# A convolution and a two-layer GELU network on one core: where the last tap is multiplied, and in which order the taps are added

## The chip, the cores and the metric

The kernel runs on one core of a Trainium2 chip. The metric is the device time of one execution in microseconds (us); smaller is better. The engines are TensorE (PE in the profile, its weight loads PEld), VectorE (DVE), ScalarE (ACT), GpSimd (POOL) and SyncE (SP, which only issues DMAs here). Each engine works through a queue of its own in the order in which the program issued its instructions, and engines wait for each other by semaphores.

## The reference

```python
w = softmax(weight, axis=-1)                      # 8 heads x 7 taps
x_pad = concat([zeros((B, 6, D)), x], axis=1)     # B = 8, S = 4096, D = 192
x = einsum('hk,bskhg->bshg', w, windows(x_pad, 7)).reshape(B * S, D)
h = x @ w_in                                      # 192 -> 2048
g = h * (1.0 / (1.0 + np.exp(-1.702 * h)))
return (g @ w_out).astype(np.float32)             # 2048 -> 192
```

A causal convolution of seven taps along the sequence, with one set of weights for every head of 24 channels, is followed by a product into 2048 columns, a GELU and a product back to 192. All is float32.

## The kernel before, in words

The 32768 tokens are taken in 32 blocks ("big" = 0 to 31) of 1024 tokens. For each block:

- **Convolution.** x is loaded by eight DMAs (`load_x`, L66) and turned by VectorE into `xt` (`transpose_x`, L439), in three groups of channels c = 0, 1, 2. From block 3 on ScalarE multiplies each of the 3 x 7 taps (`tap`, L483; the multiplication is L487). Tap 0 goes straight into the block's place in `conv_t`; the others go to "homes", pieces of the large buffer `g` that the second product has done with. The taps of c = 0 are added by accumulating DMAs (`tree`, L509); those of c = 1 and c = 2 by twelve additions on GpSimd (`next_add`, L501, the addition is L504), each into `conv_t`. Before the change these wait in a list `adds`, from which the newest is taken first. When a block's additions are issued ("done"), SP copies its block 2 across the halves of the partitions (`cross`); the other blocks and eleven sums of them (`vsum`, made by GpSimd, L363) follow later as `cross` pieces.
- **First product** (`hidden`, L763). A fast matrix scheme makes it out of 20 products for each half v = 0, 1 of the columns (`product1`, L588: the matmul at L595; each is two matmuls on 64 rows, and the trace shows each as two passes). The hand-written list `FIRST` (L643) names its items in order: "prod" on TensorE, "copy" (L630) and "gelu" (L612 from PSUM, L617 from SBUF) on ScalarE, "sum" (L636, or L363 and L361) on VectorE. Names a0 to a9 are PSUM banks handed out in turn from `free`, k0 to k6 are places in `room` (SBUF). An item's first number says whose it is: 0, this half; 1, the next half; 2, the next half's opening product 11. After the second half, items 1 belong to the next block and wait in `later`: the copy a2<-a0 is issued by `seeds_ahead` during the second product (PLAN's "final"), the rest by `rest_ahead` (L733) at the beginning of the next block's first product. So a first product begins with products 0, 4, 10, 6, 2, 13, 18, and with the copies k2<-a2 (after product 0, before product 10 writes a2 again), k6<-a0 and k1<-a9; then `FIRST` begins with its half v = 0.
- `FILL` (L659; `FILL_1`, L670, for block 1) tells what else is issued ahead of which item of `FIRST`, for each half: "add" additions, "turn" transposes of the block after next (the first of them issues whatever is left of the next block's taps and additions), "vsum", "g" the early sums of g (L361, L363, L995), "tap", "cross", and, for block 1, "work", a step of the convolution on VectorE.
- **Second product** (`second`, L1001; matmuls at L1019). It, too, is a fast scheme. The list `PLAN` (L954) is its order: "main" begins one of 20 main products of four steps (one of two), "side" appends three side products, "go" n does n steps, each one step of the main product for three column groups and one matmul of a side product beside them. When a side product ends, ScalarE copies it to `room` at once (L1044, the side copy). "seed" (L1048, ScalarE) puts a value back into PSUM, "join" (VectorE, L361 or L363) adds values, "sum" makes sums of pieces of g ("spots") on VectorE and "acc" on GpSimd's DMA queue, "turn" and "store" put out results, and "tap", "tree", "vsum" and "cross" are the next block's work. "final" gives two banks free and lets `seeds_ahead` copy a2<-a0 for the next first product.

The tap homes are spots of g: 11, 10, 16 for c = 0; 17, 14, 20 for c = 1; 15, 13, 9 for c = 2 (two taps each). So a tap can be multiplied when the second product has read that spot, and a GELU of the next first product may write the spot only when the tap has been added. `need("done n")` issues everything that block n still lacks.

In PLAN before the change 20 taps are issued up to "final" and the last, tap 6 of c = 1, right behind it. The additions are issued in FILL at the items 0, 6 and 9.

Of the kernel before, what the change touches and what calls it, by code (L numbers as in the profile page):

```python
# [15 lines left out]
def kernel(  # L16
# [80 lines left out]
    g = consts.tile([P, NG, 2, 2, NG, T], F32)  # L97
# [381 lines left out]
    TAPS_IN = (0, 2, 1)  # L479
    TREE = {2: [(1, 2)], 4: [(3, 4)], 6: [(5, 6), (0, 1), (3, 5), (0, 3)]}  # L480
    TREE_1 = {2: [(1, 2)], 4: [(3, 4), (0, 1)], 6: [(5, 6), (0, 3), (0, 5)]}

    def tap(big, c, k):  # L483

        dst = own(big)[:, 2 * c : 2 * c + 2, :]
        home = tap_home(big, c, k) if k else dst
        act.mul(home, conv_src(big, c, k), cw[:, c, k : k + 1])  # L487
        if k and c not in DMA_TAPS and big > 1:
            adds.append((dst, home))
            if big == 2:  # L490
                next_add()
            return
# [6 lines left out]
    tree, adds = [], []  # L499

    def next_add():  # L501
        if adds:
            dst, home = adds.pop()
            nc.gpsimd.tensor_add(dst, dst, home)  # L504
# [133 lines left out]
    def plain(u, m, n, v, slot, ks=range(NC), first=0):  # L638

        for k in ks:  # L640
# [20 lines left out]
            0: (("add", 4),), 6: (("add", 4),), 7: (("turn", 0),), 9: (("add", 4),), 21: (("turn", 1),),  # L661
            26: (("turn", 2),),
        },
        {
            0: (("vsum",),), 1: (("vsum",), ("vsum",)), 2: (("g", 0),), 6: (("vsum",), ("vsum",)), 8: (("vsum",),),
            12: (("vsum",),), 14: (("g", 1),), 15: (("g", 2),), 17: (("vsum",), ("vsum",)), 18: (("g", 3),),
            21: (("vsum",),), 23: (("g", 4),), 25: (("vsum",),), 35: (("cross",),),
# [4 lines left out]
            0: (("add", 12),), 4: (("tap",),), 6: (("work", 0.8),), 15: (("work", 0.8),), 16: (("work", 0.8),),  # L672
            21: (("tap",),), 23: (("tap",),), 25: (("tap",), ("work", 0.8), ("work", 0.8)), 28: (("work", 0.8),),
            32: (("tap",),), 35: (("tap",),), 38: (("tap",),), 42: (("work", 0.8),),
        },
        {
            0: (("g", 0),), 6: (("g", 1),), 19: (("g", 2), ("g", 3)), 23: (("g", 4),), 25: (("turn", 0),),
            28: (("turn", 1),), 31: (("turn", 2),),
# [259 lines left out]
    def store(big, n, o=None, queues=(nc.sync,) * 3):  # L938
# [16 lines left out]
        ("sum", 14, 14, "-", 18), ("side", 13, 16, "k0"), ("main", 1, 5, "p2", 1), ("sum", 7, 8, "-", 7), ("vsum",),  # L955
# [45 lines left out]
    def second(big, bx, bs, by, final, last):  # L1001
# [74 lines left out]
        while ready and big > 1:  # L1076
            next_tap()
# [273 lines left out]
```

## Time and profile before

| | us |
|---|---|
| median of 3 runs | 2300.35 (2299.83 to 2300.5) |
| the profiled execution | 2299.75 |
| its span, first to last instruction | 2298.0 |
| TensorE busy in it | 2271.9 |

The profile's rows give a line of the kernel, an engine and an operation, what it writes and reads by the program's own names, and the shapes. In a timeline each row is a run of like instructions: its start and length in us, their count, and in brackets the idle time of the engine just before and what ended it. "issue" there means that nothing that the profile shows was waited for. In the chain of waits a row is start, length, engine, what it writes and the line.

### The profile page before, as it was taken

The numbers are of one execution on the slowest core, as the hardware profiler recorded it, in microseconds if no ns is written. First come the engines' busy times: TensorE is split into PE (matmuls) and PEld (weight loads), VectorE is DVE, ScalarE is ACT, GpSimd is POOL, SyncE is SP. The second block draws the span as 40 slices with busy tenths as digits, with TensorE's granted clock in tenths as the row PEclk, the third lists the DMA queues.
The fourth block names the chain that finished last, engine by engine and source line by source line (L and its number), as shares of the span: only waits on it lengthen the run. The fifth ranks groups of instructions, "written<-read, shape, count | busy, mean of one in ns | idle before, by whom it ended". The sixth has DMA issues, their size and how long they took to land.

```text
span 2298.0 us, 62000 instructions
## 1 busy us (share of the span) xinstructions
PE 2271.9 (99%) x24966; PEld 1377.8 (60%) x24966; DVE 1921.3 (84%) x2842; ACT 1775.9 (77%) x3481; POOL 1100.6 (48%) x1101
## 2 busy tenths in 40 slices
PE   9899999999999999999999999999999999999999
PEld 5356656666656666566666566665666655666655
DVE  8798888888888878888888888888888888888788
ACT  8578777778877787777788777877777887778755
POOL 1445554555454555545554445555455544455510
PEclk9999999999999999999999999999999999999999
DMA  8976667656666656676566666666765667664543
GB/s 198 158 150 131 127 126 150 133 124 123 131 137 138 129 122 126 127 148 135 123 123 132 138 138 128 123 124 128 148 134 123 123 130 139 139 126 99 100 98 71
DMA packets 281072, 298.84 MB, mean 130 GB/s; under 512 B 120144, under 2 KB 212304, under 8 KB 280784
## 3 DMA queue, kind: packets, MB, share of 16 engines
q0 software_dynamic: 58080, 151.48, 36.6%
q1 hardware_dynamic: 221056, 143.00, 27.4%
q8 instruction: 197, 3.23, 0.6%
q14 instruction: 91, 0.75, 0.1%
q10 hardware_dynamic: 1648, 0.39, 0.1%
HBM read 53.15 MB, written 25.17 MB: 34 GB/s over the span
## 4 chain that ended last, share of the span: by engine, by line
PE 94%; DVE 2%; DMA 1%; ACT 1%; issue 1%; SPq 0%; DVEq 0%; ACTq 0%
PE slot L595 48%; PE slot L1019 44%; PE slot L837 1%; DMA g<-in_moe_w_in_dram 1%; DVE g L363 0%; DVE g L361 0%; PE slot L842 0%; SPq L266 0%; DMA xin<-in_x_dram 0%; ACT g L612 0%; DMA w_in_s<-in_moe_w_out_dram 0%; ACT g L487 0%; DMA conv_t<-conv_t 0%; ACT room L630 0%; ACT w_form L487 0%
## 5 line engine op out<-in xcount | busy, mean ns | idle before, releaser
L595 PE MATMUL slot<-conv_t,w_in_s 64*128 64x512 f32 x5152 | 1170.6, 599 | 8.6 <-issue 4.8
L595 PEld LDWEIGHTS slot<-conv_t,w_in_s 64*128 64x128 f32 x5152 | 728.0, 186 | 440.3 <-issue 218.6
L1019 PE MATMUL slot<-g,w_form 128*32 128x256 f32 x9672 | 895.3, 379 | 0.3 <-DVE room L363 0.3
L1019 PEld LDWEIGHTS slot<-g,w_form 128*32 128x32 f32 x9672 | 482.2, 110 | 160.3 <-DVE room L363 0.8
L636 DVE TENSOR_TENSOR slot<-slot,room 128x512 f32<-128x512 f32 x496 | 321.0, 693 | 212.3 <-ACT g L612 162.5
L504 POOL TENSOR_TENSOR conv_t<-conv_t,g 128x512 f32<-128x512 f32 x354 | 452.6, 1282 | 66.8 <-ACT g L487 43.8
L612 ACT ACTIVATE g<-slot 128x512 f32<-128x512 f32 x776 | 421.1, 613 | 77.7 <-PE slot L595 77.5
L1019 PE MATMUL slot<-g,w_out_s 128*32 128x256 f32 x5952 | 467.6, 380 | 2.9 <-DVE g L363 1.5
L363 DVE TENSOR_TENSOR g<-g 128x1024 f32<-128x1024 f32 x372 | 442.8, 1224 | 1.1
L1044 ACT COPY room<-slot 32x256 f32<-32x256 f32 x651 | 237.4, 365 | 253.7 <-PE slot L1019 242.9
L630 ACT COPY room<-slot 128x512 f32<-128x512 f32 x620 | 339.9, 611 | 31.4 <-PE slot L595 19.4
L1019 PEld LDWEIGHTS slot<-g,w_out_s 128*32 128x32 f32 x5952 | 238.9, 110 | 195.4 <-ACT g L617 23.5
L487 ACT ACTIVATE g<-xt,cw 128x512 f32<-128x512 f32 x534 | 350.7, 714 | 3.0
L363 POOL TENSOR_TENSOR conv_t<-conv_t 128x256 f32<-128x256 f32 x210 | 193.5, 929 | 232.1 <-PE slot L595 186.7
L995 POOL DMA_DIRECT2D g<-g x124 | 107.6, 943 | 352.3 <-PE slot L1019 166.6
L1019 PE MATMUL slot<-osbs,w_form 128*32 128x256 f32 x2232 | 225.3, 379 | 0.1
L509 POOL DMA_DIRECT2D g<-g x120 | 104.5, 886 | 224.4 <-DVE room L363 88.5
L630 ACT COPY slot<-slot 128x512 f32<-128x512 f32 x248 | 136.5, 572 | 54.9 <-PE slot L595 52.9
L617 ACT ACTIVATE g<-room 128x1024 f32<-128x1024 f32 x124 | 132.7, 1070 | 55.2 <-DVE room L636 55.2
L636 DVE TENSOR_TENSOR slot<-room,slot 128x512 f32<-128x512 f32 x248 | 156.3, 684 | 14.7 <-PE slot L595 13.7
L636 DVE TENSOR_TENSOR room<-slot,room 128x512 f32<-128x512 f32 x248 | 158.7, 681 | 2.5 <-ACT room L630 1.8
L361 DVE TENSOR_TENSOR room<-room 96x256 f32<-96x256 f32 x155 | 87.4, 564 | 71.1 <-ACT room L1044 70.0
(171 smaller groups left out, 1772.5 us busy)
## 6 DMA issues: line engine op xcount, KB each, us to landing
g<-g POOLq DMA_DIRECT2D x124, 512.0 KB, 5.6
xin<-in_x_dram SPq DMA_DIRECT2D x240, 180.0 KB, 4.1
conv_t<-conv_t SPq DMA_DIRECT2D x186, 192.0 KB, 2.9
g<-g POOLq DMA_DIRECT2D x120, 256.0 KB, 4.5
out_dram<-osbs SPq DMA_DIRECT2D x186, 128.0 KB, 2.8
conv_t<-conv_t SPq DMA_DIRECT2D x124, 128.0 KB, 2.5
g<-room POOLq DMA_DIRECT2D x31, 512.0 KB, 5.5
conv_t<-g POOLq DMA_DIRECT2D x60, 256.0 KB, 4.2
```

What stands on the lines that cost most here:

```text
L363: eng.tensor_sub(v(dst), v(a), v(b))
L487: act.mul(home, conv_src(big, c, k), cw[:, c, k : k + 1])
L504: nc.gpsimd.tensor_add(dst, dst, home)
L509: nc.gpsimd.dma_start(out=out, in_=src, accum_op=ALU.add)
L595: nc.tensor.matmul(slot[h], w_in_s[halves[h], a, v * P : (v + 1) * P], src, start=first, stop=True, skip_group_check=True,)
L612: act.activation(dst[:, :, h, :], src[h].rearrange("p (o t) -> p o t", o=2), AF.Gelu_apprx_sigmoid, scale=float(sign),)
L617: act.activation(dst.rearrange("p o h t -> p h o t"), src.rearrange("p h (o t) -> p h o t", o=2), AF.Gelu_apprx_sigmoid, scale=float(sign),)
L630: act.copy(bank(dst, h), bank(src, h))
L636: op(*(bank(t, h) for t in (dst, a, b)))
L995: nc.gpsimd.dma_start(out=spot(dst), in_=spot(a), accum_op=ALU.add)
L1019: nc.tensor.matmul(dst, w, t, start=first, stop=last, skip_group_check=True)
L1044: act.copy(to, d)
```

## The change

Three things are altered. The last of a block's 21 taps is no longer issued in the second product: `second` now leaves two entries in `ready` (that tap and its label), and FILL issues the tap ahead of item 2 of the next `FIRST`, so behind the copies k2, k6 and k1 and the first GELU on ScalarE. The additions are no longer taken newest first but in the order of a list, `ADDS_IN`, that begins with the last tap. And the orders in `FIRST`, `FILL`, `FILL_1` and `PLAN` are written anew around that.

```diff
     TAPS_IN = (0, 2, 1)
+    ADDS_IN = [(1, 6), (2, 5), (2, 6), (2, 1), (2, 2), (2, 3), (2, 4)] + [(1, k) for k in range(1, 6)]
...
         if k and c not in DMA_TAPS and big > 1:
-            adds.append((dst, home))
+            adds.append((ADDS_IN.index((c, k)), dst, home))
+            adds.sort(key=lambda a: a[0])
...
         if adds:
-            dst, home = adds.pop()
+            _, dst, home = adds.pop(0)
             nc.gpsimd.tensor_add(dst, dst, home)
...
     FIRST = [
-        (0, "sum", "a3", "a4", "-", "k1"), (0, "gelu", 2, 1, "a0", 1), (0, "copy", "k0", "a2", 1),
...
+        (0, "gelu", 2, 1, "a0", 1), (0, "sum", "a3", "a4", "-", "k1"), (0, "copy", "k0", "a2", 1),
...
     FILL = [
         {
-            0: (("add", 4),), 6: (("add", 4),), 7: (("turn", 0),), 9: (("add", 4),), 21: (("turn", 1),),
-            26: (("turn", 2),),
+            2: (("tap",), ("add", 4)), 3: (("add", 4),), 4: (("add", 4),), 5: (("turn", 0),), 26: (("turn", 1),),
+            29: (("turn", 2),),
         },
         {
-            0: (("vsum",),), 1: (("vsum",), ("vsum",)), 2: (("g", 0),), 6: (("vsum",), ("vsum",)), 8: (("vsum",),),
-            12: (("vsum",),), 14: (("g", 1),), 15: (("g", 2),), 17: (("vsum",), ("vsum",)), 18: (("g", 3),),
-            21: (("vsum",),), 23: (("g", 4),), 25: (("vsum",),), 35: (("cross",),),
+            0: (("g", 0),), 1: (("vsum",), ("vsum",), ("vsum",)), 3: (("vsum",), ("vsum",)), 5: (("vsum",),),
+            13: (("g", 1), ("vsum",)), 19: (("g", 2), ("g", 3), ("vsum",), ("vsum",)), 21: (("vsum",),),
+            24: (("vsum",),), 25: (("g", 4),), 37: (("cross",),),
         },
     ]
     FILL_1 = [
         {
-            0: (("add", 12),), 4: (("tap",),), 6: (("work", 0.8),), 15: (("work", 0.8),), 16: (("work", 0.8),),
-            21: (("tap",),), 23: (("tap",),), 25: (("tap",), ("work", 0.8), ("work", 0.8)), 28: (("work", 0.8),),
-            32: (("tap",),), 35: (("tap",),), 38: (("tap",),), 42: (("work", 0.8),),
+            0: (("add", 12),), 2: (("work", 0.8),), 8: (("tap",),), 14: (("work", 0.8),), 15: (("work", 0.8),),
+            19: (("tap",),), 21: (("tap",),), 22: (("work", 0.8),), 27: (("tap",),), 28: (("work", 0.8),),
+            29: (("work", 0.8),), 32: (("tap",),), 35: (("tap",),), 42: (("work", 0.8), ("tap",)),
         },
...
     PLAN = [
...
-        ("sum", 13, 18, "+", 4), ("acc", 7, 10), ("go", 1), ("join", "k7", "k1", "+", "k6"), ("acc", 18, 14),
-        ("side", 8, 8, "k1", 2, 4), ("sum", 20, 20, "-", 11), ("main", 2, 5, "p4", 0), ("sum", 6, 9, "-", 5),
-        ("acc", 12, 9), ("vsum",), ("go", 4), ("main", 20, 0, "p1", 0), ("go", 1), ("cross",), ("go", 1),
-        ("join", "k2", "k7", "-", "p4"), ("side", 6, 13, "k8"), ("cross",), ("tap",), ("tap",), ("tree",), ("go", 1),
-        ("sum", 15, 15, "-", 16), ("join", "k2", "k2", "-", "p2"), ("go", 1), ("main", 9, 6, "p4", 0), ("vsum",),
...
+        ("side", 8, 8, "k1", 2, 4), ("main", 2, 5, "p4", 0), ("vsum",), ("go", 2), ("sum", 6, 9, "-", 5), ("go", 2),
+        ("main", 20, 0, "p1", 0), ("go", 1), ("cross",), ("go", 1), ("join", "k2", "k7", "-", "p4"),
+        ("sum", 20, 20, "-", 11), ("acc", 12, 9), ("side", 6, 13, "k8"), ("go", 1), ("join", "k2", "k2", "-", "p2"),
+        ("go", 1), ("main", 9, 6, "p4", 0), ("vsum",), ("tap",), ("tap",), ("tap",), ("go", 2), ("tap",), ("tree",),
+        ("go", 1), ("sum", 15, 15, "-", 16), ("join", "k9", "p1", "+", "k5"), ("tap",), ("tap",), ("go", 1),
+        ("join", "k10", "p0", "-", "k9"), ("main", 3, 15, "p2", 0), ("cross",), ("go", 1), ("sum", 5, 7, "+", 15),
...
-        ("turn", 1, 0, 0, "k6"), ("store", 0, 0), ("main", 24, 19, "p5", 0), ("final",), ("tap",), ("go", 2),
...
+        ("final",), ("cross",), ("go", 2), ("join", "k1", "p3", "-", "k3"), ("go", 1), ("join", "k2", "p2", "-", "k4"),
...
     ]
...
-        while ready and big > 1:
+        while len(ready) > 2 and big > 1:
             next_tap()
         end_taps()
```

The items of `FIRST` are the same 43, put in another order. Queue by queue, that order is the old one on TensorE, ScalarE and VectorE; what changes with it is which filling stands ahead of which item. "g" 0 is the Vector sum 6 = 6 - 10; before, it stands between the sums a3 and a5 of the second half, and after the change ahead of both. In the second product the side copies and the taps come in other groups on ScalarE: between the side copy at the 46th step and the copy a2<-a0 they were 3, 1, 4, 4, 4 and 1 taps (the first three stand ahead of that side copy) and are 3, 3, 2, 2, 3, 3 and 1.

More of the change, by code (lines that the diff above doesn't have):

```diff
@@ L671 @@
         {
-            0: (("add", 12),), 4: (("tap",),), 6: (("work", 0.8),), 15: (("work", 0.8),), 16: (("work", 0.8),),
-            21: (("tap",),), 23: (("tap",),), 25: (("tap",), ("work", 0.8), ("work", 0.8)), 28: (("work", 0.8),),
-            32: (("tap",),), 35: (("tap",),), 38: (("tap",),), 42: (("work", 0.8),),
-        },
-        {
-            0: (("g", 0),), 6: (("g", 1),), 19: (("g", 2), ("g", 3)), 23: (("g", 4),), 25: (("turn", 0),),
-            28: (("turn", 1),), 31: (("turn", 2),),
+            0: (("add", 12),), 2: (("work", 0.8),), 8: (("tap",),), 14: (("work", 0.8),), 15: (("work", 0.8),),
+            19: (("tap",),), 21: (("tap",),), 22: (("work", 0.8),), 27: (("tap",),), 28: (("work", 0.8),),
+            29: (("work", 0.8),), 32: (("tap",),), 35: (("tap",),), 42: (("work", 0.8), ("tap",)),
+        },
+        {
+            1: (("g", 0),), 6: (("g", 1),), 15: (("g", 2),), 19: (("turn", 0), ("g", 3)), 23: (("g", 4),),
+            26: (("turn", 1),), 31: (("turn", 2),),
         },
@@ L954 @@
     PLAN = [
-        ("sum", 14, 14, "-", 18), ("side", 13, 16, "k0"), ("main", 1, 5, "p2", 1), ("sum", 7, 8, "-", 7), ("vsum",),
[18 rows of a table removed]
-        ("sum", 5, 7, "+", 15), ("go", 1), ("main", 21, 7, "p2", 0), ("tap",), ("tap",), ("tap",), ("tap",), ("go", 1),
-        ("tree",), ("go", 1), ("sum", 6, 14, "+", 6), ("side", 7, 20, "k1"), ("vsum",), ("vsum",), ("go", 1),
[6 rows of a table removed]
-        ("main", 15, 12, "p2", 0), ("tap",), ("tap",), ("tap",), ("tree",), ("go", 1), ("tap",), ("go", 1),
[3 rows of a table removed]
-        ("turn", 1, 0, 0, "k6"), ("store", 0, 0), ("main", 24, 19, "p5", 0), ("final",), ("tap",), ("go", 2),
[3 rows of a table removed]
+        ("sum", 14, 14, "-", 18), ("side", 13, 16, "k0"), ("main", 1, 5, "p2", 1), ("vsum",), ("tap",), ("go", 1),
[15 rows of a table added]
+        ("go", 1), ("main", 9, 6, "p4", 0), ("vsum",), ("tap",), ("tap",), ("tap",), ("go", 2), ("tap",), ("tree",),
[3 rows of a table added]
+        ("go", 2), ("side", 7, 20, "k1"), ("vsum",), ("vsum",), ("tree",), ("go", 1), ("sum", 6, 6, "-", 17),
+        ("tree",), ("go", 1), ("main", 10, 14, "p0", 0), ("tap",), ("tap",), ("tree",), ("tree",), ("go", 2),
[10 rows of a table added]
+        ("turn", 0, 0, 1, "k1"), ("store", 0, 1), ("go", 1), ("turn", 0, 1, 1, "k2"), ("store", 1, 1),
+        ("join", "k1", "p5", "+", "k5"), ("turn", 0, 1, 0, "k1"), ("join", "k8", "k8", "+", "k0"),
+        ("turn", 1, 1, 0, "k8"), ("store", 1, 0),
     ]
```

69 rows, old and new, of tables (FIRST, PLAN) are left out of this document.

## The prediction

> **What bounds the kernel now.** First the page, for the engine that is never free, and the chain that ended last, in order of time.
>
> ```profile
> span 2298.0 us, 62000 instructions
> PE 2271.9 (99%) x24966; PEld 1377.8 (60%) x24966; DVE 1921.3 (84%) x2842; ACT 1775.9 (77%) x3481; POOL 1100.6 (48%) x1101
> ```
>
> ```profile
> 187.01 36.06 PE slot L595 x157
> ...
> 293.29 33.81 PE slot L1019 x624
> 327.27 36.23 PE slot L595 x156
> ...
> 397.48 36.23 PE slot L595 x156
> ```
>
> TensorE carries the chain from 187 us to the end: a first product (L595) and a second product (L1019) for each of the blocks 2 to 31. One period is 397.48 - 327.27 = 70.21 us. So the change can only pay where TensorE waits inside that period, and 29 times over. A busy TensorE is not one at its peak, so I look at its weight loads, beside ScalarE, where one first product begins.
>
> ```profile
> 326.72 0.38 PE L1019 MATMUL slot<-g,w_form 128*32 128x256 f32 x1
> 327.27 4.23 PE L595 MATMUL slot<-conv_t,w_in_s 64*128 64x512 f32 x15 [0.18 <-issue]
> ```
>
> ```profile
> 329.46 0.29 PEld L595 LDWEIGHTS slot<-conv_t,w_in_s 64*128 64x128 f32 x2 [0.59 <-ACT room L630]
> ...
> 330.43 0.25 PEld L595 LDWEIGHTS slot<-conv_t,w_in_s 64*128 64x128 f32 x2 [0.18 <-issue]
> ```
>
> ```profile
> 326.61 1.06 ACT L630 COPY slot<-slot 128x512 f32<-128x512 f32 x2
> 327.69 0.72 ACT L487 ACTIVATE g<-xt,cw 128x512 f32<-128x512 f32 x1
> 328.44 0.36 ACT L1044 COPY room<-slot 32x256 f32<-32x256 f32 x1
> 328.83 1.07 ACT L630 COPY room<-slot 128x512 f32<-128x512 f32 x2
> ...
> 334.06 1.07 ACT L630 COPY room<-slot 128x512 f32<-128x512 f32 x2 [0.35 <-PE slot L595]
> ```
>
> In ScalarE's queue stand: the copy a2<-a0 for which product 0 waits (326.61), then the last tap (L487, 327.69), the last side copy (L1044), and the copy k2<-a2 (328.83). The third product, 10 into a2, may not write a2 before k2 is taken out; its load stands 0.59 us on "ACT room L630" and begins at 329.46. All that lies between is the tap's 0.72 us and ScalarE's queue.
>
> The trace holds the same place without any taps, because after block 31 there is no further input:
>
> ```profile
> 2223.30 0.38 PE L1019 MATMUL slot<-g,w_form 128*32 128x256 f32 x1
> 2223.61 0.70 PE L595 MATMUL slot<-conv_t,w_in_s 64*128 64x512 f32 x2
> ```
>
> ```profile
> 2223.77 0.36 ACT L1044 COPY room<-slot 32x256 f32<-32x256 f32 x1 [0.28 <-PE slot L1019]
> 2224.76 2.05 ACT L630 COPY room<-slot 128x512 f32<-128x512 f32 x4 [0.63 <-PE slot L595]
> ...
> 2228.50 1.09 ACT L612 ACTIVATE g<-slot 128x512 f32<-128x512 f32 x2
> ```
>
> ```profile
> 2225.40 0.29 PEld L595 LDWEIGHTS slot<-conv_t,w_in_s 64*128 64x128 f32 x2 [0.64 <-ACT room L630]
> ...
> 2226.37 0.25 PEld L595 LDWEIGHTS slot<-conv_t,w_in_s 64*128 64x128 f32 x2 [0.18 <-issue]
> ```
>
> Counted from the first matmul of the stage, the load that follows the two bound ones stands at 330.43 - 327.27 = 3.16 us there and at 2226.37 - 2223.61 = 2.76 us here. That is **0.40 us** a period. The stage also begins sooner: 0.31 us after the last matmul of the second product instead of 0.55, because ScalarE was not behind with its taps. That 0.24 us is a second, separate prize.
>
> **The change part by part.** Expanded item by item, FIRST gives TensorE, ScalarE and VectorE the same order as before; only the fillings between its items and the positions in PLAN differ. No instruction is added or dropped.
>
> *The last tap.* It goes from ahead of k2 to behind k2, k6, k1 and the first GELU (item 2 of FILL). In the tapless block the side copy ends at 2224.13 and k2 starts at 2224.76, 1.15 us after the stage's start, released by TensorE. With the tap away, k2 gets there too, as long as the copies a2<-a0, which come just ahead, stand as they do now (with the tap away, copies and side copy end at 326.61 + 1.06 + 0.36 and two gaps, 0.8 us after the stage's start). I take 0.40 us; bounds 0 and 0.45. At its new place the tap lies in the 0.35 us that ScalarE idles before 334.06, so k0 comes about 0.3 us late; k0 frees the bank for product 16, four products later, and no term results.
>
> *The taps inside the second product.* This decides when a2<-a0 can start. ScalarE runs without a real pause from the tap at 312.01 to 326.61:
>
> ```profile
> 312.01 1.95 ACT L487 ACTIVATE g<-xt,cw 128x512 f32<-128x512 f32 x3
> 313.87 0.35 ACT L1044 COPY room<-slot 32x256 f32<-32x256 f32 x1
> 314.13 0.72 ACT L487 ACTIVATE g<-xt,cw 128x512 f32<-128x512 f32 x1
> 315.07 0.37 ACT L1044 COPY room<-slot 32x256 f32<-32x256 f32 x1 [0.23 <-PE slot L1019]
> ...
> 315.73 2.56 ACT L487 ACTIVATE g<-xt,cw 128x512 f32<-128x512 f32 x4
> 318.32 0.75 ACT L1044 COPY room<-slot 32x256 f32<-32x256 f32 x2
> ```
>
> ```profile
> 308.56 2.35 DVE L363 TENSOR_TENSOR g<-g 128x1024 f32<-128x1024 f32 x2
> 310.83 0.41 DVE L363 TENSOR_TENSOR room<-room,slot 96x256 f32<-96x256 f32 x1
> 311.16 1.22 DVE L363 TENSOR_TENSOR g<-g 128x1024 f32<-128x1024 f32 x1
> ```
>
> Seventeen taps, eight side copies and two seeds stand there before and after; only their grouping changes, from 3, 1, 4, 4, 4, 1 taps to 3, 3, 2, 2, 3, 3, 1. A run of four taps costs 2.56 us, so 0.61 a further tap; from a tap's start to a copy's are 0.63 us ahead of 313.87 and 0.75 ahead of 318.32; from a copy's to a tap's 0.26 behind 313.87, up to 0.4 where the copy ends first. One group of taps more trades one step of 0.61 and one between copies (0.38) for one of 0.63 to 0.75 and one of 0.26 to 0.4: 0.1 us at most. The 0.23 us pause at 315.07 goes, since that copy now comes two taps later. Against that, the Vector sum 20 = 20 - 11, now one of the two at 308.56, moves behind the join at 310.83. It then takes the place at 311.16 and ends about 312.3, and the first tap overwrites spot 11, so it waits for it: 0.3 us late at the head. Net 0.3 - 0.23 = 0.07; I take **0.05 us late**, bounds 0.24 early (the tapless start) and 0.6 late (every step at its dearer price, the head late by half a microsecond). Sum 15 follows at about 312.6 and ends at 313.8, just as the product that reads spot 15 is due (49th of 78 steps from 293.29 at 33.81 / 78 = 0.43 us: about 314.1); no cost taken, 0.1 at worst.
>
> *The additions.* They wait for the last tap and then run without a break:
>
> ```profile
> 328.50 16.05 POOL L504 TENSOR_TENSOR conv_t<-conv_t,g 128x512 f32<-128x512 f32 x12 [1.70 <-ACT g L487]
> ```
>
> ```profile
> 351.34 0.73 POOL L363 TENSOR_TENSOR conv_t<-conv_t 128x256 f32<-128x256 f32 x1 [3.58 <-PE slot L595]
> ```
>
> ```profile
> 2246.42 1.18 ACT L612 ACTIVATE g<-slot 128x512 f32<-128x512 f32 x2
> ```
>
> In the tapless block the first GELU ends 5.98 us into the stage (2228.50 + 1.09); plus the tap 0.72 and the 0.09 between tap and addition, they run from 6.8 to 22.85 us instead of 1.2 to 17.3. The cover is GpSimd's idle time: one sum stands between the additions and the one at 351.34, 24.1 us in, which waits 3.58 us for TensorE. Taps are written into g, so the order decides who waits next: (2,5) and (2,6), which free spot 9 for a GELU of the first half, end at 6.8 + 3 x 1.34 = 10.8 us (now they are seventh and eighth and end at 11.9, and no GELU waits); (1,4), the eleventh, frees spot 14 by 21.5, and the GELU that writes there starts at 2246.42, 22.8 us in. Queued behind the additions on SP are the cross copy of block 2, which product 38 of 40 reads some 33 us in (0.9 us each), and eight loads of x for the next period. So I count nothing, with 1.3 us of margin.
>
> *The collision.* VectorE's sum 6 = 6 - 10 moves ahead of sum a3 in the second half, into the 1.11 us before it:
>
> ```profile
> 2244.24 1.30 DVE L636 TENSOR_TENSOR slot<-slot,room 128x512 f32<-128x512 f32 x2 [1.30 <-ACT g L612]
> 2246.66 1.30 DVE L636 TENSOR_TENSOR slot<-slot,room 128x512 f32<-128x512 f32 x2 [1.11 <-ACT room L630]
> ```
>
> It will be issued 21.85 us in, just ahead of the end of the first row (2245.54 - 2223.61 = 21.93), while the twelfth addition (21.6 to 22.85) runs. What that does is shown at 328.83, where a sum of two SBUF operands meets the first addition, against the same sum in the tapless block:
>
> ```profile
> 328.83 1.20 DVE L361 TENSOR_TENSOR room<-room 96x256 f32<-96x256 f32 x1 [0.79 <-ACT room L1044]
> ```
>
> ```profile
> 2224.55 0.38 DVE L361 TENSOR_TENSOR room<-room 96x256 f32<-96x256 f32 x1
> ```
>
> 1.20 against 0.38 us: VectorE stood until GpSimd's addition was over. The addition ends at about 328.50 + 1.27 = 329.77 (16.05 / 12 = 1.34 less a gap of 0.07), and the sum 0.26 us later, so 0.12 us of it had passed while it stood. So sum 6, 1.22 us long like that at 311.16, ends at about 22.85 + 1.1 = 23.95, and sum a3, 1.30 us, at 25.2 instead of 24.35. TensorE's load at 2250.33, below, is 26.7 us in and belongs to product 16; product 17 stands two products earlier, at about 24.9. Price **0.2 us** (a part is lost in TensorE's other half), bounds 0 (sum 6 gets the port first and the addition waits) and 0.35. The Trainium skill, "SBUF — State Buffer", section "SBUF: two separate sides", calls it an exclusive lock: whoever starts first has the port for its whole instruction. By that sum 6 would take its full 1.22 us behind the addition, 0.1 us more than I read from the rows: 0.3 us a period, and 2297.4 in all. Where a3 is first, as now, the later product 16 waits:
>
> ```profile
> 2249.55 0.49 PEld L595 LDWEIGHTS slot<-conv_t,w_in_s 64*128 64x128 f32 x3 [0.24 <-issue]
> 2250.33 0.29 PEld L595 LDWEIGHTS slot<-conv_t,w_in_s 64*128 64x128 f32 x3 [0.30 <-DVE slot L636]
> ```
>
> 0.30 against 0.24: that 0.05 us goes.
>
> *The start* (blocks 0 and 1, up to 187 us) is bound by ScalarE and then VectorE with the same instructions; the shuffled FILL_1 I take at 0, plus or minus 1.5 us.
>
> **The sum.** 0.40 + 0.05 - 0.05 - 0.20 = 0.20 us a period, times 29 is 5.8 us. The profiled execution took 2299.75 us, 1.75 us more than its span; less 5.8 it is 2293.95. The median of the runs is 0.6 us above it, so I forecast 2294.5.
>
> **Rivals.**
> - *No collision* (sum 6 gets the port first, or the additions end sooner): 0.40 a period, 11.6 us, 2288.7. For it: a quarter of a microsecond decides. Against: the twelfth addition starts ahead in my count.
> - *Given back at the start of the stage.* ScalarE reaches a2<-a0 about 0.25 us late and the collision costs its 0.2: 0 a period, 2300. For it: there is no slack at all in that queue.
> - *Slower.* The taps' queue ends 0.6 us late, because the sum 20 = 20 - 11 holds its head and each change of kind costs the dearer step: 0.25 - 0.6 = -0.35 us a period, 10 us, 2310.5. It decides from 0.25 us on. Against: the rows' steps cancel.
> - *ScalarE early.* The stage begins 0.24 us sooner as in the tapless block, without collision: 0.64 times 29 = 18.6 us, 2281.8. Against: seventeen taps still stand ahead.
>
> **How the numbers follow.** Forecast 0.36, no collision 0.24, given back 0.20, slower 0.12, early 0.08. The forecast's own spread (2291 to 2298) crosses the bound of 0.2%, 2295.75 us, about what a measurement of this kernel can tell from no change; three quarters of it lie below. Faster: 0.27 + 0.24 + 0.08 = 0.59; same: 0.09 + 0.20 = 0.29; slower 0.12. The range leaves out the early and the slower case, with the start's 1.5 us and the unsettled ScalarE steps at the ends of the others: 2285 to 2304.
>
> **What would show it.** Right: no wait of 0.59 us on "ACT room L630" at the third product; the load after it 2.76 us into the stage; the tap behind the first GELU; additions from 6.8 to 22.9 us; sum 6 of 2.1 us with a wait of product 17 on VectorE. Wrong: the stage beginning over 0.65 us after the second product's last matmul, GELUs of the second half waiting for GpSimd, or TensorE waits at the 49th step of the second product.

## The result, and the profile after

The changed kernel takes 2293.39 us in the median of 8 runs (2291.46 to 2295.5), the kernel before 2300.43 us on the same chip (8 runs): a ratio of 0.9971, 95% interval 0.996 to 0.9982. The profiled execution took 2292.87 us, its span is 2291.2 us. In the lines below the helpers have moved: the first product's matmul is L597, the second's L1021, the copies are L632, the GELUs L614 and L619, the side copies L1046, the taps L488, the additions L506, the bank sums L638.

First the page, then two periods of the chain:

```profile
span 2291.2 us, 61944 instructions
...
PE 2258.2 (99%) x24966; PEld 1373.4 (60%) x24966; DVE 1916.1 (84%) x2842; ACT 1768.0 (77%) x3481; POOL 1096.9 (48%) x1101
```

```profile
396.88 35.77 PE slot L597 x155
432.65 33.85 PE slot L1021 x624
466.51 0.31 issue
466.82 35.76 PE slot L597 x155
```

TensorE still carries the chain, with a period of 466.82 - 396.88 = 69.94 us instead of 70.21. Over all 29 periods from block 2 on, the median goes from 70.22 to 69.92 us. Three stretches of a period move: the first product, from its first matmul's start to its last's, from 35.64 to 35.17 us (-0.47); the second product from 33.51 to 33.54 (+0.03); and the way from its last matmul to the next stage, +0.13. That last one stands in TensorE's timeline:

```profile
396.20 0.38 PE L1021 MATMUL slot<-g,w_form 128*32 128x256 f32 x1
396.88 4.67 PE L597 MATMUL slot<-conv_t,w_in_s 64*128 64x512 f32 x19 [0.30 <-issue]
```

396.88 - 396.20 = 0.68 us instead of 0.55. The weight loads and ScalarE at the same place:

```profile
398.65 0.29 PEld L597 LDWEIGHTS slot<-conv_t,w_in_s 64*128 64x128 f32 x2 [0.17 <-ACT room L632]
399.14 0.29 PEld L597 LDWEIGHTS slot<-conv_t,w_in_s 64*128 64x128 f32 x3 [0.19 <-ACT room L632]
399.62 0.24 PEld L597 LDWEIGHTS slot<-conv_t,w_in_s 64*128 64x128 f32 x2 [0.18 <-issue]
```

```profile
396.21 1.06 ACT L632 COPY slot<-slot 128x512 f32<-128x512 f32 x2
397.30 0.36 ACT L1046 COPY room<-slot 32x256 f32<-32x256 f32 x1
398.01 2.05 ACT L632 COPY room<-slot 128x512 f32<-128x512 f32 x4 [0.35 <-PE slot L597]
...
401.75 1.09 ACT L614 ACTIVATE g<-slot 128x512 f32<-128x512 f32 x2
402.72 0.73 ACT L488 ACTIVATE g<-xt,cw 128x512 f32<-128x512 f32 x1
```

The 0.59 us on "ACT room" is gone; where the bracket still names it, it holds 0.17 to 0.19 us, no more than the 0.18 of the free loads. The load after the two bound ones stands 399.62 - 396.88 = 2.74 us into the stage, for the 2.76 forecast. k2 (398.01) now waits for TensorE and not behind a tap, and the tap follows the first GELU. GpSimd, VectorE and the loads in the second half, for the collision:

```profile
403.53 15.88 POOL L506 TENSOR_TENSOR conv_t<-conv_t,g 128x512 f32<-128x512 f32 x12 [5.70 <-ACT g L488]
```

```profile
418.71 1.78 DVE L363 TENSOR_TENSOR g<-g 128x1024 f32<-128x1024 f32 x1
420.42 1.28 DVE L638 TENSOR_TENSOR slot<-slot,room 128x512 f32<-128x512 f32 x2
```

```profile
421.76 1.24 PEld L597 LDWEIGHTS slot<-conv_t,w_in_s 64*128 64x128 f32 x7 [0.18 <-DVE slot L638]
```

Sum 6 takes 1.78 us where it takes 1.22 alone, so it did meet the twelfth addition, which ends at 403.53 + 15.88 = 419.41. But the sum behind it is done at 421.70 and the load that needs it, product 17's, starts at 421.76 after 0.18 us, the ordinary distance: TensorE loses nothing.

Two things are new. The span moved by 6.8 us, while 29 periods at 0.294 make 8.5. Added up by stage starts: block 2 begins at 184.75 us instead of 186.94 (-2.2), the 29 medians give -8.5, what single periods are longer than the median grows from 0.4 to 4.3 (+3.9), and the tail is the same (-0.1): -6.9. The scattered stalls are of two kinds. In block 2's first product 1.2 us go, because TensorE waits for a cross copy:

```profile
189.76 5.62 DMA conv_t<-conv_t
```

SyncE issued that copy behind the stores of block 1's results and ahead of this stage's loads, so the loads that follow are not its cause. In the second products 3.0 us go (0.1 before): 1.1 and 1.0 in blocks 3 and 8, and smaller pieces. In block 8 the chain of waits leaves TensorE for a DMA and two sums:

```profile
637.40 9.08 DMA g<-osbs
...
647.64 2.37 DVE g L363 x2
...
650.05 4.95 PE slot L1021 x87
```

The page has a row for this second kind, on VectorE; in the kernel before it reads "1.1" after the second bar:

```profile
L363 DVE TENSOR_TENSOR g<-g 128x1024 f32<-128x1024 f32 x372 | 465.0, 1265 | 17.6 <-DMA g<-osbs 15.1
```

VectorE's sums now wait 15.1 us in all for an accumulating DMA, "acc" 8 <- 0; most of that VectorE has to spare. The list of DMAs (count, size, median us from issue to landing), before and then after:

```profile
conv_t<-conv_t SPq DMA_DIRECT2D x186, 192.0 KB, 2.9
...
g<-osbs POOLq DMA_DIRECT2D x30, 512.0 KB, 4.5
```

```profile
conv_t<-conv_t SPq DMA_DIRECT2D x186, 192.0 KB, 5.6
...
g<-osbs POOLq DMA_DIRECT2D x30, 512.0 KB, 7.6
```

and SyncE's queue in one first product, before (it begins at 467.69) and after (466.82):

```profile
472.40 5.71 SPq L523 DMA_DIRECT2D conv_t<-conv_t  x4
485.29 3.82 SPq L78 DMA_DIRECT2D xin<-in_x_dram  x8
```

```profile
470.88 19.59 SPq L525 DMA_DIRECT2D conv_t<-conv_t  x4
490.56 4.05 SPq L78 DMA_DIRECT2D xin<-in_x_dram  x8
```

The loads of x are issued 23.7 us into the stage instead of 17.6, behind a cross copy that waits for the additions. So they and the cross copies behind them meet that accumulation, which is issued 31 us in: in the median the last load lands 1.8 us after the accumulation's issue, where before it lands 5.5 us ahead of it. Experiments have to tell whether this is the cause or beside it.

### The profile page after: what moved, and what is told of

The parts are those of the page before. It is cut to its first block, busy times and chain, and to the rows that moved or that the text cites. A ratio compares the mean times of both kernels' runs of the same rounds, so it can differ in the third digit from the quotient of the medians.

```text
span 2291.2 us, 61944 instructions
## 1 busy us (share of the span) xinstructions
PE 2258.2 (99%) x24966; PEld 1373.4 (60%) x24966; DVE 1916.1 (84%) x2842; ACT 1768.0 (77%) x3481; POOL 1096.9 (48%) x1101
## 4 chain that ended last, share of the span: by engine, by line
PE 91%; DVE 3%; DMA 3%; issue 2%; ACT 1%; SPq 1%; POOL 0%; DVEq 0%; ACTq 0%; POOLq 0%
PE slot L597 46%; PE slot L1021 44%; DMA g<-osbs 1%; DVE g L363 1%; DMA conv_t<-conv_t 1%; DMA g<-in_moe_w_in_dram 1%; PE slot L839 0%; SPq L266 0%; DMA conv_t<-w_form 0%; DMA xin<-in_x_dram 0%; DMA w_in_s<-in_moe_w_out_dram 0%; ACT g L614 0%; DVE w_in_s L363 0%; DVE g L361 0%; DVE xt L443 0%
## 5 line engine op out<-in xcount | busy, mean ns | idle before, releaser
L597 PE MATMUL slot<-conv_t,w_in_s 64*128 64x512 f32 x5152 | 1155.4, 598 | 13.1 <-issue 8.6
L597 PEld LDWEIGHTS slot<-conv_t,w_in_s 64*128 64x128 f32 x5152 | 725.7, 186 | 431.9 <-issue 220.3
L1021 PE MATMUL slot<-g,w_form 128*32 128x256 f32 x9672 | 897.0, 379 | 0.0
L1021 PEld LDWEIGHTS slot<-g,w_form 128*32 128x32 f32 x9672 | 481.5, 110 | 159.5 <-issue 0.4
L506 POOL TENSOR_TENSOR conv_t<-conv_t,g 128x512 f32<-128x512 f32 x354 | 450.7, 1279 | 211.5 <-ACT g L488 190.7
L638 DVE TENSOR_TENSOR slot<-slot,room 128x512 f32<-128x512 f32 x496 | 320.4, 691 | 201.1 <-ACT g L614 119.2
L363 DVE TENSOR_TENSOR g<-g 128x1024 f32<-128x1024 f32 x372 | 465.0, 1265 | 17.6 <-DMA g<-osbs 15.1
L614 ACT ACTIVATE g<-slot 128x512 f32<-128x512 f32 x776 | 423.2, 612 | 71.5 <-PE slot L597 71.4
L1021 PE MATMUL slot<-g,w_out_s 128*32 128x256 f32 x5952 | 468.3, 380 | 3.7 <-DVE g L363 2.9
L1046 ACT COPY room<-slot 32x256 f32<-32x256 f32 x651 | 237.4, 365 | 246.1 <-PE slot L1021 229.5
L488 ACT ACTIVATE g<-xt,cw 128x512 f32<-128x512 f32 x534 | 354.1, 715 | 15.0 <-DVE g L363 12.8
L632 ACT COPY room<-slot 128x512 f32<-128x512 f32 x620 | 337.2, 614 | 31.2 <-PE slot L597 30.9
L1021 PEld LDWEIGHTS slot<-g,w_out_s 128*32 128x32 f32 x5952 | 237.2, 110 | 200.6 <-ACT g L619 23.5
L363 POOL TENSOR_TENSOR conv_t<-conv_t 128x256 f32<-128x256 f32 x210 | 216.0, 1037 | 73.1 <-DVE osbs L361 48.6
L1021 PE MATMUL slot<-osbs,w_form 128*32 128x256 f32 x2232 | 225.9, 379 | 0.1
L632 ACT COPY slot<-slot 128x512 f32<-128x512 f32 x248 | 136.1, 572 | 55.8 <-PE slot L597 54.7
L638 DVE TENSOR_TENSOR slot<-room,slot 128x512 f32<-128x512 f32 x248 | 159.5, 689 | 22.9 <-PE slot L597 22.4
L638 DVE TENSOR_TENSOR room<-slot,room 128x512 f32<-128x512 f32 x248 | 158.6, 680 | 22.8 <-ACT room L632 22.8
L619 ACT ACTIVATE g<-room 128x1024 f32<-128x1024 f32 x124 | 132.8, 1071 | 55.8 <-DVE room L638 55.8
L1021 PEld LDWEIGHTS slot<-osbs,w_form 128*32 128x32 f32 x2232 | 117.1, 110 | 42.8 <-ACT room L1050 0.6
```

What stands on the lines that cost most here:

```text
L363: eng.tensor_sub(v(dst), v(a), v(b))
L597: nc.tensor.matmul(slot[h], w_in_s[halves[h], a, v * P : (v + 1) * P], src, start=first, stop=True, skip_group_check=True,)
L614: act.activation(dst[:, :, h, :], src[h].rearrange("p (o t) -> p o t", o=2), AF.Gelu_apprx_sigmoid, scale=float(sign),)
L619: act.activation(dst.rearrange("p o h t -> p h o t"), src.rearrange("p h (o t) -> p h o t", o=2), AF.Gelu_apprx_sigmoid, scale=float(sign),)
L632: act.copy(bank(dst, h), bank(src, h))
L638: op(*(bank(t, h) for t in (dst, a, b)))
```

## The experiments

Of each, the median, the ratio to runs of the kernel before on the same chip, and the median period.

| kernel | us | ratio (95%) | period | scattered | in second products |
|---|---|---|---|---|---|
| before | 2300.43 |  | 70.22 | 0.4 | 0.1 |
| changed | 2293.39 | 0.9971 (0.996 to 0.9982) | 69.92 | 4.3 | 3.0 |
| tap alone | 2291.34 | 0.9957 (0.9944 to 0.9969) | 69.80 | 3.1 | 2.6 |
| tap back | 2304.91 | 1.0014 (1.0004 to 1.0023) | 70.33 | 3.3 | 0.0 |
| old order of additions | 2344.18 | 1.0187 (1.0173 to 1.0201) | 71.83 | 0.0 | 0.1 |
| sum 6 back | 2294.55 | 0.9973 (0.9962 to 0.9984) | 69.96 | 2.1 | 1.2 |
| sum 20 ahead | 2290.1 | 0.9951 (0.9938 to 0.9963) | 69.75 | 5.1 | 4.5 |
| loads first | 2290.17 | 0.9954 (0.9941 to 0.9966) | 69.91 | 0.3 | -0.1 |
| block 1 as before | 2295.41 | 0.9972 (0.996 to 0.9983) | 69.92 | 4.7 | 2.9 |
| sum 20 and loads | 2286.0 | 0.9932 (0.9919 to 0.9944) | 69.75 | 0.4 | 0.0 |
| sum 20, additions ahead | 2286.0 | 0.9933 (0.992 to 0.9945) | 69.75 | 0.6 | 0.0 |
| two taps | 2309.12 | 1.0032 (1.0021 to 1.0044) | 70.60 | 1.3 | 0.0 |
| two taps, transpose behind | 2279.06 | 0.9901 (0.9884 to 0.9917) | 69.53 | 1.0 | 0.0 |

"Scattered" is what the 29 periods of the profiled execution are longer than their median, summed; the last column is the same for the 29 second products alone. The former holds single stalls of first products too, block 2's above all, which come and go between profiles (0 to 1.6 us).

**The tap alone**, in the kernel before:

```diff
+    ADDS_IN = [(1, 6), (2, 5), (2, 6), ...]          # and the two edits that use it
-            0: (("add", 4),), 6: (("add", 4),), ...
+            2: (("tap",), ("add", 4)), 6: (("add", 4),), ...
-        ... ("final",), ("tap",), ("go", 2),
+        ... ("final",), ("go", 2),
-        while ready and big > 1:
+        while len(ready) > 2 and big > 1:
```

> The kernel before, with only the last tap moved behind the first GELU of the next first product, and with the fixed order of the additions; all sums, taps inside the second product and the fillings of blocks 0 and 1 stay as before. Theory A, the tap's place in ScalarE's queue is the whole of the steady gain: the third product's load no longer waits 0.59 us on ACT room, the first-product stage is 0.42 us shorter, the stage still begins 0.55 us after the second product's last matmul (nothing holds the head of the taps), and the wait of 0.05 us of product 16 stays: 29 x 0.42 = 12.2 us off, 2288.2 us. Theory A with B, the later additions hold SyncE's queue and so crowd the transfers: some 3 us of the 12.2 are given back in single periods, 2291 to 2292 us. Rival, the gain comes from the regrouped second product and the shuffled start: no more than 2 us off, 2298 to 2300 us.

Its period is 69.80 us, 0.42 less than before: the first product lasts 35.22 us, the second 33.51, the stage begins 0.55 us after the last matmul. The period is theory A's to the hundredth, and 3.1 us of scattered stalls come with it, 2.6 of them in second products, which is about B's number. So the steady gain is the tap's place, and all the rest of the change takes 69.92 - 69.80 = 0.12 us a period away again.

**The tap back**, in the changed kernel:

```diff
-            2: (("tap",), ("add", 4)), 3: (("add", 4),), ...
+            0: (("add", 4),), 3: (("add", 4),), ...
-        ("final",), ("cross",), ("go", 2), ...
+        ("final",), ("tap",), ("cross",), ("go", 2), ...
-        while len(ready) > 2 and big > 1:
+        while ready and big > 1:
```

> The changed kernel with the last tap back ahead of the copies of the next first product, its additions from the first item on; the rest as changed. Theory A: the 0.59 us on ACT room returns and each first-product stage is 0.42 us longer, 2293.4 + 12.2 = 2305.6 us. Theory A with B: the additions end 5.6 us earlier again, SyncE issues the loads of x at 17.6 us into the stage instead of 23.8, the accumulation 8<-0 lands in about 4.5 us again and the scattered stalls of 3.4 us in all go: about 2302 us. Rival, the gain is the regrouping's and the start's: 2293 to 2295 us.

The period is 70.33 us: 0.41 more than the changed kernel, and 0.11 more than the kernel before, which again is the price of the regrouping. The accumulation lands in 4.5 us (median) and no second product of the blocks 3 to 29 is over 33.6 us long, so that class of stalls goes, as B says. The time of 2304.91 is still above B's 2302. The profiled execution (2306.91 us) has 3.3 us of other stalls, all in first products; the two largest, 1.7 us (block 5) and 0.9 (block 21), are told under the hardware below.

**The old order of the additions**, in the changed kernel (newest first, with `adds.pop()`):

> The changed kernel, its additions newest first as before instead of in the fixed order; the last tap stays at its new place. Theory, the order is what lets the tap move: the additions (2,6) and (2,5) come seventh and eighth and end about 17.3 us into the stage instead of 10.8, so the GELU of the first half that writes their spot, due about 13.5 us in, stands 3 to 4 us on GpSimd; ScalarE catches up only part of that, TensorE loses 1 to 3 us a period: 2320 to 2380 us. Rival, ScalarE's slack in the first half covers it or the GELU in question comes later: 2293.4 us.

```profile
413.22 1.09 ACT L613 ACTIVATE g<-slot 128x512 f32<-128x512 f32 x2
416.59 1.08 ACT L613 ACTIVATE g<-slot 128x512 f32<-128x512 f32 x2 [2.27 <-POOL conv_t L505]
```

One GELU of each first half waits 2.27 us for an addition, and the first product lasts 37.08 us instead of 35.17: 29 x 1.91 = 55 us. The median is only 50.8 us above the changed kernel's, because this profile has no scattered stalls: here the last load has landed 3.8 us before the accumulation is issued (median), and the accumulation takes 4.5 us. The GELU waited less than the 3 to 4 us expected; the place, the cause and the order of size are right. The fixed order belongs to the move: without it the kernel is 1.9% slower than the one before.

**Sum 6 back** behind the sum a3 of the second half:

```diff
-            0: (("g", 0),), 1: (("vsum",), ("vsum",), ("vsum",)), 3: ...
+            1: (("vsum",), ("vsum",), ("vsum",)), 2: (("g", 0),), 3: ...
```

> The changed kernel with VectorE's sum 6 = 6 - 10 back behind the sum a3 of the second half. The prediction's term: the collision with the twelfth addition costs 0.2 us a period and the wait of product 16 is worth 0.05, so without both 29 x 0.15 = 4.4 us off, 2289.0 us. Theory D, the collision is there but product 17 comes late enough to cover it: nothing is won, product 16 waits its 0.05 us again, a period of 69.97 instead of 69.92, 2294.9 us; sum 6 takes 1.2 us instead of 1.8.

The period is 69.96 us, the first product 35.22: the 0.05 us of product 16 come back and nothing is won. Sum 6 takes 1.22 us here. Theory D holds; the prediction's collision term was nothing.

**Sum 20 ahead** of the join:

```diff
-        ("side", 8, 8, "k1", 2, 4), ("main", 2, 5, "p4", 0), ...
-        ... ("join", "k2", "k7", "-", "p4"), ("sum", 20, 20, "-", 11), ("acc", 12, 9), ...
+        ("side", 8, 8, "k1", 2, 4), ("sum", 20, 20, "-", 11), ("main", 2, 5, "p4", 0), ...
+        ... ("join", "k2", "k7", "-", "p4"), ("acc", 12, 9), ...
```

> The changed kernel with VectorE's sum 20 = 20 - 11 of the second product back ahead of the join k2 = k7 - p4. Theory C, this sum alone holds the first of the run of taps: the first tap starts 0.3 to 0.37 us sooner after the second product's start, the copies a2<-a0 follow, the stage begins 0.55 us instead of 0.68 after the last matmul: 29 x 0.13 = 3.8 us off, 2289.6 us; at most 0.3 a period, 2285 us. Rival, the regrouping of taps and side copies makes the copies late, or the pause that came back takes the gain: 2293.4 us, within 1 us.

ScalarE's head of the taps in the changed kernel, and with this edit:

```profile
381.06 0.37 ACT L1046 COPY room<-slot 32x256 f32<-32x256 f32 x1 [0.47 <-PE slot L1021]
381.82 1.95 ACT L488 ACTIVATE g<-xt,cw 128x512 f32<-128x512 f32 x3 [0.40 <-DVE g L363]
```

```profile
380.07 0.36 ACT L1046 COPY room<-slot 32x256 f32<-32x256 f32 x1 [0.47 <-PE slot L1021]
380.46 1.96 ACT L488 ACTIVATE g<-xt,cw 128x512 f32<-128x512 f32 x3
...
395.05 1.06 ACT L632 COPY slot<-slot 128x512 f32<-128x512 f32 x2
```

The wait on VectorE goes, the stage begins 0.56 us after the last matmul and the second product is back at 33.50: a period of 69.75, 0.17 less. That is theory C with 0.04 more, because the second product's 0.04 was this sum's too. It is the lowest steady period so far, while the scattered stalls stay (5.1 us). The head starts 0.37 us sooner and the stage only 0.13, because part of the rival is true as well: from the first tap to the copy a2<-a0 ScalarE takes 396.21 - 381.82 = 14.39 us in the changed kernel and 395.05 - 380.46 = 14.59 here, as much as the 14.60 before the change (326.61 - 312.01). So small waits of 0.2 us return when the head is on time.

**Loads first.** The cross copy of block 2 is put on a list when the additions are issued, and taken from it right behind the eight loads:

```diff
-            cross(big, OPEN, OPEN + 1)
+            open_cross.append(big)                    # from token block 3 on; earlier ones at once, as before
...
                     load_x(big + 3)
+            if args[0] == NC - 1:
+                while open_cross:
+                    cross(open_cross.pop(0), OPEN, OPEN + 1)
```

> The changed kernel with one move in SyncE's queue: the cross copy of block 2, which waits for the additions, is issued behind the eight loads of x instead of ahead of them. Theory B: the loads are issued at about 17.6 us into the first-product stage again and are done when the accumulation 8<-0 begins; that lands in about 4.5 us (median) instead of 7.6, VectorE's second sum of the second product waits no more for it, and the scattered stalls (1 us in blocks 3 and 8, smaller ones in six others, 3.4 us in all) go: 2290.0 us. Rival, the stalls are chance, or come from the later cross copy itself: 2293.4 us, with as many stalls at other places.

SyncE's queue in the first product that begins at 465.24 us, and the DMA:

```profile
469.32 1.31 SPq L525 DMA_DIRECT2D conv_t<-conv_t  x2
483.08 3.82 SPq L78 DMA_DIRECT2D xin<-in_x_dram  x8
487.80 17.61 SPq L525 DMA_DIRECT2D conv_t<-conv_t  x14
```

```profile
g<-osbs POOLq DMA_DIRECT2D x30, 512.0 KB, 4.5
```

The loads go out 17.8 us into the stage, the accumulation lands in 4.5 us, no second product of the blocks 3 to 29 is longer than 33.55, and the scattered sum falls from 4.3 to 0.3 us at the same period. The additions end as late as in the changed kernel; only the queue differs. So the stalls in the second products come from SyncE's queue and not from chance. The thirteen profiles agree: in the five in which the last load lands 1.7 to 2.0 us after the accumulation's issue (medians) the accumulation takes 7.4 to 7.7 us and second products lose 1.2 to 4.5 us; in the eight in which the load lands at least 3.8 us ahead, it takes 4.5 us and they lose 0.1 us at most. Of the 4.0 us by which the scattered sum falls, 3.0 are of this kind; the 0.9 by which block 2's stall in its first product is smaller here are not shown to be this edit's, which leaves that copy as it was.

**Block 1 as before**: the old `FIRST` and `FILL_1` for block 1 alone.

> The changed kernel with the old fillings and the old written order of the first product's items for block 1 alone. If the fillings of block 1 were worth something by themselves, the first product of block 1 (it ends at 147.6 us in the changed kernel, at 148.6 in the kernel before) ends 1 us later and the whole takes 2294.5 us; if what block 1 gains is its second product's (37.25 us instead of 38.4, the same new grouping of taps as in every block), that stays at 37.25 and the whole within 0.7 us of 2293.4.

The second product of block 1 begins at 149.4 us here; with the old fillings it does so at 148.6 (before) and 149.8 (tap alone), with the new ones anywhere from 147.5 to 150.6 in the ten other profiles. It lasts 37.5 us, near the new 37.25 and not the old 38.4. So about 1 us of the start is that second product's; whether the fillings give the 2295.41 - 2293.39 = 2.0 us, or part of it, these runs don't tell, since the ratios' intervals are nearly the same.

**Both gains together**, sum 20 ahead and loads first:

> Both edits that gained by themselves: sum 20 = 20 - 11 ahead of the join, and the loads of x ahead of the cross copy in SyncE's queue. If their causes are apart (the head of the taps; the transfers' crowd), the gains add: periods of 69.75 us without the 5.5 us of scattered stalls that the run with sum 20 alone still showed, 2290.1 - 5 = 2285 us. If they share a cause: 2289 to 2290 us.

2286.0 us, the period 69.75 and 0.4 us scattered: they add, as causes that are apart do.

**Additions ahead**, another road to the same, with sum 20 ahead:

```diff
-    ADDS_IN = [(1, 6), (2, 5), ..., (2, 4)] + [(1, k) for k in range(1, 6)]
+    ADDS_IN = [(2, 5), ..., (2, 4)] + [(1, k) for k in range(1, 7)]
-            2: (("tap",), ("add", 4)), 3: ...
+            0: (("add", 4),), 2: (("tap",),), 3: ...
```

> Sum 20 = 20 - 11 ahead of the join, and the last tap's addition put last instead of first, so that the eleven others run from the start of the stage; SyncE's order as changed. Theory B by another road: the additions end about 17 us into the stage instead of 22.5, the loads go out at 17.6, the scattered stalls go and sum 6 meets no addition: 2285 us, as with the loads moved. Rival, the additions at the start of the stage stand in VectorE's way there, or hold what the first products need: 2290 us or more.

2286.0 us as well. The additions run from 396.10 to 412.47 us, the accumulation lands in 4.5 us, and SyncE's order is untouched. It wasn't needed that the last tap's addition be the first.

**Two taps moved**, on top of the kernel with the additions ahead. If the stage's start hangs on the taps in front of a2<-a0, one tap less there must give it:

```diff
-            0: (("add", 4),), 2: (("tap",),), 3: (("add", 4),), ...
+            0: (("add", 4),), 2: (("tap",),), 3: (("tap",), ("add", 4)), ...
-        ... ("join", "k6", "k6", "+", "p4"), ("tap",), ("go", 1),
+        ... ("join", "k6", "k6", "+", "p4"), ("go", 1),
-        while len(ready) > 2 and big > 1:
+        while len(ready) > 3 and big > 1:
```

> Sum 20 = 20 - 11 ahead of the join, and the last two taps of the queue moved: the tap (1,5) behind the first GELU of the next first product, (1,6) behind the copy k0, the additions (1,5) and (1,6) last of the twelve. Theory E, the stage's start hangs on nothing but ScalarE's queue: with one tap of 0.62 us less ahead of the copies a2<-a0 it begins 0.31 us after the second product's last matmul, as in the block without taps, instead of 0.56; 29 x 0.25 = 7.2 us less than with the additions ahead alone, a period of 69.50 us, 2278.8 us. Rival, the two taps behind the first GELU make the GELUs of the first half late and TensorE waits for their banks, or the copies then wait for TensorE: 2283 us or more.

Half right: the stage begins 0.31 us after the last matmul in every block. But the first product lasts 36.27 us, 1.10 more, nearly all of it at product 16 of the first half. The chain there (start, length, what):

```profile
402.72 0.96 ACT room L632 x2
403.68 0.63 ACT g L488
404.31 0.02 issue
404.33 0.78 DVE xt L443
405.11 0.60 DVE slot L638
405.71 0.04 issue
405.75 14.39 PE slot L597 x62
```

Neither the GELUs nor the bank of k0 hold TensorE. VectorE's transpose (L443) overwrites the `xt` that the last tap reads; it waits for the tap, and the sum a5, which product 16 needs, stands behind the transpose in VectorE's queue.

**The transpose behind the sum a5**, on top of the two taps:

```diff
-            ... 4: (("add", 4),), 5: (("turn", 0),), 26: ...
+            ... 4: (("add", 4),), 7: (("turn", 0),), 26: ...
```

> The two taps moved as in the run before, and VectorE's transpose of x (L443), which overwrites what the last tap reads, moved from ahead of the sum a5 to behind it. Theory F: the 1.10 us a period that the two taps cost came from this transpose alone, which stood 1.31 us on the tap with the sum a5 = k1 - a1 behind it in VectorE's queue, while product 16 waited for a5. With the sum ahead of it the stage starts 0.31 us after the last matmul and lasts 35.2 us again: a period of 69.50 us, 2278.8 us. Rival, the two taps hold the GELUs and the bank of k0 as well: some of the 1.10 us stays, 2283 us or more; or the transpose is late for the sum a6 behind it and the same wait shows one product later, 2300 us.

```profile
401.86 1.29 DVE L638 TENSOR_TENSOR slot<-room,slot 128x512 f32<-128x512 f32 x2 [0.42 <-PE slot L597]
403.06 0.77 DVE L443 STREAM_TRANSPOSE xt<-xin 128x576 f32<-128x576 f32 x1
```

```profile
464.14 35.72 PE slot L597 x157
499.86 33.81 PE slot L1021 x624
533.66 6.34 PE slot L597 x26
```

The period is 533.66 - 464.14 = 69.52 us, the time 2279.06, a ratio of 0.9901 (0.9884 to 0.9917) to the kernel before: theory F, and the fastest kernel here.

## Why the prediction was right, and where not

2294.5 us were forecast and 2293.39 measured, inside the forecast's own spread; but the sum is right partly because its misses cancel.

| step, us a period | forecast | found |
|---|---|---|
| third product's wait, tap behind the first GELU | -0.40 | -0.42 |
| product 16, second half | -0.05 | -0.05 |
| a2<-a0 late | +0.05 | +0.17 |
| collision of sum 6 | +0.20 | 0 |
| sum | -0.20 | -0.30 |
| start, in all | 0 (1.5 either way) | -2.2 in one execution, about 1 shown |
| transfers into second products, in all | 0 | +2.8 |
| other single stalls, in all | 0 | +1.1, of which block 2's first product 1.2 |

Over 29 periods the sum is 2.7 us better than forecast and the start 2.2, and the single stalls take 3.9 back. That these come to within 1.1 us of the forecast is luck; that the tap's place was worth 0.40 is not.

- **The last tap.** Taken from the block without taps, by rows; found in the changed kernel and, alone and undone, in two experiments (0.42 and 0.41). The same reading gives the stage's start of 0.31 us, which the forecast kept as a rival: it needed one tap less and not none.
- **a2<-a0.** The mechanism, sum 20 in the place where the first tap needs it, is shown by moving it. It was only sized too small. The forecast: 0.3 late less the pause of 0.23, rounded to 0.05. Measured: the head is 0.37 us late, the queue behind it 0.20 shorter (14.39 us for 14.59), so a2<-a0 is 0.17 late. Of this 0.13 show at the stage's start and 0.04 in the second product. With 0.68 us the stage's start even passed the 0.65 that the forecast had named as a sign of being wrong. The pause is no gain by itself: with the head on time the regrouped queue takes 14.59 us again.
- **The collision.** It happens as forecast, sum 6 at 21.83 us into the stage for 21.85. The step that failed is its price. The tap began 0.1 us sooner and the additions took 15.88 us instead of 16.05, so they end 22.53 us in for 22.85, and the sum a3 ends 24.8 us in for 25.2, just when product 17 is due at 24.9. A third of a microsecond in the end of twelve additions was the whole term, inside the bounds (0 to 0.35); the rival "no collision" had the right price and half of the reason: the additions did end sooner, but the collision stayed, 1.78 us for sum 6 where 2.1 were forecast.
- **SyncE's queue.** The forecast names what is queued behind the additions, the cross copy and the eight loads, and then counts nothing, because it asked only whether these come in time for their own readers. They do. What it left out is whom they meet: the accumulation 8 <- 0 on another queue, read by the second sum of the next second product. This is the failed step on the transfers, 2.8 us, and every experiment that has the loads landed before that accumulation takes it away.
- **The start** was put at 0 with 1.5 us. Of the 2.2 us between the two profiles about 1 us, in block 1's second product, is in every profile with the new grouping; the rest is within the scatter of single executions. Block 2's stall of 1.2 us then takes as much back in this profile. It is in some of the profiles and not in others, and why is open.
- **The rivals' other side.** "Slower" was to decide at 0.25 us of lateness in that queue; the head was late by more, 0.37, but the pause took up 0.20 of it, and only 0.13 reached the stage's start.

The Trainium skill, "SBUF — State Buffer", section "SBUF: two separate sides", would have had sum 6 run its full 1.22 us after the addition, to 419.41 + 1.22 = 420.63; it ended at 418.71 + 1.78 = 420.49. The row-based 1.1 us after the addition (1.08 measured) was nearer. On the transfers, "DMA: Bandwidth & Descriptors", section "Issuing engines are not separate DMA queues", says that DMAs started by ScalarE, SyncE or GpSimd run on the same 16 DMA engines and interleave; the 4.5 us that become 7.6 when SyncE's loads and copies meet GpSimd's accumulation agree.

## What to carry to other kernels

When work is moved later on one engine, follow each queue behind it to the next transfer, and ask what that transfer will share the DMA engines with, not only whether it is in time for its reader. Look also at what overwrites the moved instruction's input, for that waits too, with its whole queue behind it. And where a stretch of the same trace runs without the suspected work, as the last block here, its numbers are the best forecast to be had.

## What the runs showed of the hardware

A VectorE sum of two SBUF operands can end only behind the second of two GpSimd additions in a row. With the tap back, block 5's stage has

```profile
400.99 2.76 DVE L361 TENSOR_TENSOR room<-room 96x256 f32<-96x256 f32 x1 [0.91 <-ACT room L1046]
403.79 0.44 DVE L937 STREAM_TRANSPOSE osbs<-room 96x256 f32<-96x256 f32 x1
```

```profile
400.67 5.56 POOL L506 TENSOR_TENSOR conv_t<-conv_t,g 128x512 f32<-128x512 f32 x4
```

where the same sum takes 0.38 us in the last block, without additions, and 1.20 us in 26 others. In this block the second addition is recorded from 401.90, before the first ends at 402.25; it ends at 403.46, and the sum 0.29 us later. In block 21 the sum took 2.56 us and the two records overlap by 0.16 us; in the 26 other blocks they overlap by only 0.03, in the kernel before they stand 0.08 apart, and in both the sum ends 0.28 us after the first addition. The two blocks are those with stages 1.7 and 0.9 us longer. Why the sum doesn't get in between there stays open.
